# One written order for five engines: windowed attention and two gated layers on one core

## The chip, the cores and the metric

The kernel runs on one core of a Trainium2 chip. The core has a matmul engine (TensorE, PE in the profile, with its weight loads as PEld), a vector engine (VectorE, DVE), an activation engine (ScalarE, ACT), a general engine (GpSimd, POOL) and a queue that issues the transfers (SyncE, SP). Each engine works through its own list of instructions; between engines they wait for one another by semaphores. The metric is the device time of one execution in microseconds (us), lower is better; several runs are taken and their median stands.

## The reference

Two batches of 768 positions go through three stages one after the other: attention over chunks of 32 positions with a small context and 8 memory keys, a layer with a position-mixing gate, and a layer with a 3-tap convolution and a sigmoid gate. All inputs are f32.

```
# attention, 8 heads of 64: chunk of 32, 16 to the left, 8 to the right, 8 memory keys
scores = scale * matmul(q_c, k_full.T); scores -= max(scores)
a = exp(scores); a /= sum(a) + 1e-9; out_c = matmul(a, v_full)
# first layer
h = gelu_tanh(x @ w_in)                  # [2, 768, 512] @ [512, 1024]
u, v = h[..., :512], h[..., 512:]
v_n = (v - mean(v)) / sqrt(var(v) + 1e-6) * g_ln
v_s = einsum('ts,bsd->btd', w_sg, v_n) + b_sg[None, :, None]
x = x + (u * v_s) @ w_out
# second layer
h = relu(x @ w_in2)                      # [2, 768, 512] @ [512, 1024]
gate = sigmoid(conv over 3 positions of h with conv_w)
y = (h * gate) @ w_out2
```

Note that `einsum('ts,bsd->btd')` mixes all 768 positions of one batch: the mix of a batch needs the normalised v of all its positions, and no others.

## The kernel before

**Tiles and stages.** The 1536 positions are cut into 12 tiles of 128; tiles 0 to 5 are batch 0, tiles 6 to 11 batch 1. For a tile, `qk` makes the scores on PE (64 small f32 matmuls), `rows_max` takes the maximum off on DVE, `ex` is the exponential on ACT, `pt` turns the result, `pv` multiplies by the values, `x_of` divides by the sum, `xt` turns the tile once more. From then on every f32 product is made of three f16 products: each operand is scaled by a power of two found from its own absolute sums (`abs_sum`, `top_of`, `scale_from`), and `split` makes a high half (ACT) and a low half (DVE, or POOL for the pieces listed in `PC`, `PX` and `PK`). `mm3` (line 157) issues the three matmuls. `V` is the v half of `x @ w_in` (12 matmuls of 512 columns a tile), `U` the u half (48 of 128 columns), `N` the normalising of three tiles, `M` the mix (18 matmuls of 384 columns for each of 16 pieces), `O` the product with w_out (12 of 384 columns, 16 pieces), `I` the product with w_in2 and its convolution (24 of 384 columns, 16 pieces), `G` the scale of a batch's gate, `H` its split (one 768-column block a piece, 8 pieces a batch) and `Y` the last product (24 of 512 columns for each of 12 tiles).

**Weights.** They arrive as 64-bit floats; `narrow` makes f32 of a 128x512 piece by three DVE operations that follow from each other (lines 105, 107, 109). There are 28 such pieces.

**Order.** Two strings, `FIRST` and `SECOND`, give the order in which steps are recorded; what the engines then get is decided by a scheduler (`schedule_with_timeline_sim=True`) on all engines but SP, which keeps the written order. The weights of the second half (`w_out`, `w_in2`, `w_out2`) are recorded as `jobs` that `pump` deals out between the steps of `SECOND`. `FIRST` holds the attention, V, U and N of all 12 tiles; after it a pool of PSUM banks and a pool of attention buffers are closed (`p1.close()`) and others take their place, and the transfer of `b_sb` behind that point, with the raw weights of the second half after it, waits until the closed buffers are free. `SECOND` runs the M and O of both batches, then the I, G, H and Y.

## Time and profile before

| what | value |
|---|---|
| runs | 389.77 us median of 3 (389.65 to 391.6) |
| the profiled execution | 391.75 us, of which 389.0 us span from the first to the last instruction |
| PE, DVE, ACT, POOL busy | 334.4, 236.5, 219.5, 74.4 us |
| PE instructions | 3658 matmuls |
| moved by DMA | 35.22 MB |

Read it so: the span is what the program itself takes; the 2.75 us beside it lie before the first and after the last instruction. A busy engine is not one at its peak: PE's records overlap, and the granted clock of its matmuls has two levels, 1.2 and 2.4 GHz, shown as a share of the upper one.

### The profile page before, as it was taken

How to read it: one execution, taken by the hardware profiler on the slowest of the kernel's cores; microseconds unless marked ns; L12 is line 12 of the kernel's file. 1: busy time of each engine (PE TensorE's matmuls, PEld its weight loads, DVE VectorE, ACT ScalarE, POOL GpSimd, SP SyncE). 2: the span in 40 equal slices, each digit the busy share in tenths (PEclk: the TensorE clock that was granted, in tenths of full speed). 3: DMA queues.
4: the chain of work that ended last, by engine and by line, in shares of the span. 5: the costliest groups of instructions: out<-in, count | busy, mean ns of one | idle time of the engine just before them, and what ended most of it. 6: DMA issues, size and time to landing. Idle time of an engine off the chain costs nothing.

```text
span 389.0 us, 8771 instructions
## 1 busy us (share of the span) xinstructions
PE 334.4 (86%) x3658; PEld 205.3 (53%) x3658; DVE 236.5 (61%) x467; ACT 219.5 (56%) x439; POOL 74.4 (19%) x194
## 2 busy tenths in 40 slices
PE   6357789949489799799999999999984999997996
PEld 6233356748347366366666665666641455553445
DVE  1983656222864153649988889969998964338000
ACT  1456556863825555345554669689669773447111
POOL 1026204401600054333000105401006100000000
PEclk9658899978969899899999999999996999998999
DMA  7994072671012002530330410510210010000021
GB/s 268 406 369 131 3 241 63 245 252 29 31 56 56 2 3 85 174 112 0 110 108 2 163 56 1 167 51 0 70 41 0 2 55 29 27 27 29 27 81 54
DMA packets 13783, 35.22 MB, mean 91 GB/s; under 512 B 1968, under 2 KB 2224, under 8 KB 13744
## 3 DMA queue, kind: packets, MB, share of 16 engines
q1 hardware_dynamic: 13744, 34.67, 25.5%
q8 instruction: 28, 0.46, 0.5%
q14 instruction: 11, 0.09, 0.1%
HBM read 31.52 MB, written 3.15 MB: 89 GB/s over the span
## 4 chain that ended last, share of the span: by engine, by line
PE 54%; DVE 16%; DMA 11%; ACT 10%; issue 4%; POOL 3%; SPq 1%; ACTq 0%; DVEq 0%
PE o L157 20%; PE mx L157 12%; PE vps L157 8%; PE i L157 5%; PE ups L157 4%; DMA raw<-in_w_out_dram 3%; DMA sgVS<-in_w_sgt_dram 2%; DMA ruWSG<-in_w_in_dram 2%; DMA vwa<-in_vw_dram 2%; DVE c L690 2%; ACT h L686 1%; DVE wsg L149 1%; DVE gate L695 1%; PE pv L296 1%; DVE c L692 1%
## 5 line engine op out<-in xcount | busy, mean ns | idle before, releaser
L157 PE MATMUL o<-wp,gsp 128*128 128x512 f16 (+1 forms) x312 | 66.0, 371 | 6.9 <-ACT gsp L143 6.9
L157 PE MATMUL i<-x2s,wi 128*128 128x384 f16 x384 | 66.9, 332 | 0.0
L157 PE MATMUL vps<-win,xs 128*128 128x512 f16 x144 | 42.7, 437 | 13.6 <-ACT xs L143 9.8
L157 PEld LDWEIGHTS <-wi 128*128 128x128 f16 x384 | 38.1, 99 | 27.5 <-issue 3.2
L157 PEld LDWEIGHTS <-gsp 128*128 128x128 f16 x312 | 30.8, 99 | 40.0 <-ACT gsp L143 8.0
L157 PE MATMUL mx<-wsg,vs 128*128 128x384 f16 x288 | 50.3, 331 | 0.0
L157 PEld LDWEIGHTS <-vs 128*128 128x128 f16 x288 | 28.3, 99 | 18.9 <-issue 1.4
L157 PE MATMUL ups<-xs,win 128*128 128x128 f16 x576 | 37.9, 222 | 0.0
L157 PEld LDWEIGHTS <-win 128*128 128x128 f16 x576 | 35.0, 100 | 4.3 <-issue 1.0
L157 PE MATMUL o<-gs,wo 128*128 128x384 f16 x192 | 34.6, 326 | 0.6 <-ACT gs L143 0.5
L157 PEld LDWEIGHTS <-xs 128*128 128x128 f16 x144 | 13.7, 108 | 30.7 <-ACT xs L143 12.0
L690 DVE SCALAR_TENSOR_TENSOR c<-h,cw_sb,c 128x768 f32<-128x768 f32 x16 | 16.3, 1017 | 16.9 <-ACT c L689 16.9
L361 DVE BATCH_NORM_STATS2 st<-v 128x6 f32<-128x512 f32 x12 | 8.3, 691 | 27.7 <-ACT v L359 27.7
L157 PEld LDWEIGHTS <-wo 128*128 128x128 f16 x192 | 18.6, 98 | 12.0 <-issue 0.2
L694 ACT ACTIVATE c<-c 128x768 f32<-128x768 f32 x16 | 13.4, 838 | 12.8 <-DVE c L692 12.8
L695 DVE TENSOR_TENSOR gate<-h,c 128x768 f32<-128x768 f32 x16 | 15.3, 956 | 8.5 <-ACT c L694 8.5
L720 ACT ACTIVATE o<-o,ixp0t 128x256 f32<-128x256 f32 x12 | 5.6, 470 | 21.8 <-issue 18.0
L359 ACT ACTIVATE v<-vps,ixv 128x512 f32<-128x512 f32 x12 | 8.2, 686 | 17.2 <-PE vps L157 17.1
L692 DVE SCALAR_TENSOR_TENSOR c<-h,cw_sb,c 128x768 f32<-128x768 f32 x16 | 16.3, 1017 | 0.7
L135 ACT ACTIVATE gs<-uf 128x384 f16<-128x384 f32 x16 | 8.3, 519 | 14.3 <-DVE uf L652 14.3
L135 ACT ACTIVATE xs<-xx 128x512 f16<-128x512 f32 x12 | 7.6, 629 | 13.3 <-DVE xx L311 13.3
L391 POOL TENSOR_TENSOR vs<-v,vs 128x512 f16<-128x512 f32 x12 | 14.1, 1193 | 5.3 <-ACT vs L390 5.3
(421 smaller groups left out, 567.3 us busy)
## 6 DMA issues: line engine op xcount, KB each, us to landing
raw<-in_w_out_dram SPq DMA_DIRECT2D x12, 512.0 KB, 3.5
vwSTG<-in_vw_dram SPq DMA_DIRECT2D x8, 520.0 KB, 3.7
raw<-in_w_in_dram SPq DMA_DIRECT2D x8, 512.0 KB, 3.5
q<-in_qt_dram SPq DMA_DIRECT2D x12, 256.0 KB, 5.3
kwb<-in_kw_dram SPq DMA_DIRECT2D x8, 368.0 KB, 6.1
out_dram<-o SPq DMA_DIRECT2D x11, 256.0 KB, 2.0
vwa<-in_vw_dram SPq DMA_DIRECT2D x4, 520.0 KB, 5.2
ruWSG<-in_w_in_dram SPq DMA_DIRECT2D x4, 512.0 KB, 9.9
```

The costliest lines, as they stand in the source:

```text
L135: nc.scalar.activation(room, src, AF.Abs, scale=2.0 ** (1 - EXP_TOP), accum_out=acc)
L149: nc.vector.scalar_tensor_tensor(out=lo, in0=src, scalar=sc[:, 0:1], in1=hi, op0=ALU.mult, op1=ALU.subtract)
L157: nc.tensor.matmul(ps, a, b, start=(i == 0), stop=(i == n - 1))
L296: nc.tensor.matmul(po[c * CH:(c + 1) * CH, par, hp * (D + 1):(hp + 1) * (D + 1)], t[rows, hp, c * CH:(c + 1) * CH], vw_t[i][rows, c, hp, : ...
L359: nc.scalar.activation(v, ps_t.pop(("v", i)), AF.Gelu_apprx_tanh, scale=inv_of(sc_x[i], i, "v"))
L361: nc.vector.bn_stats(out=st, in_=v)
L391: nc.gpsimd.tensor_tensor(out=lo[:, ib, :], in0=v, in1=hi[:, ib, :], op=ALU.subtract)
L690: nc.vector.scalar_tensor_tensor(out=c, in0=h[:, 0:S], scalar=cw_sb[:, f, 0:1], in1=c, op0=ALU.mult, op1=ALU.add)
L692: nc.vector.scalar_tensor_tensor(out=c, in0=h[:, 2:S + 2], scalar=cw_sb[:, f, 2:3], in1=c, op0=ALU.mult, op1=ALU.add)
L694: nc.scalar.activation(c, c, AF.Sigmoid)
L695: nc.vector.tensor_tensor(out=gate[b][f // 4][:, f % 4], in0=h[:, 1:S + 1], in1=c, op=ALU.mult)
L720: nc.scalar.activation(o[:, cs], ps[:, cs.start - cols.start:cs.stop - cols.start], AF.Copy, scale=inv_of(sc_g["gate", b], f"t{b}", f"p{h}"))
```

## The change

The kernel is rewritten around one table. `ORDER` is a string of some 1200 steps; `run` records each as it comes, all engines keep the recorded order (`manual_schedule()` without a list, and no scheduler), and each step is smaller than before: a step holds the work of one engine on one piece (`v.2.0` is the first three matmuls of V of tile 2, `cn.v.2` the narrowing of one piece of w_in's v half, `ms`/`mg`/`ma` the three operations behind a mix, `za` to `zd` the four behind the gate's scale). The mark `@` names the memory slot: PSUM is four single banks M0 to M3 and two pairs D0 and D1 for the whole program, and SBUF slots are reused by name, so nothing is closed in the middle. What the table does with the order:

- It goes batch by batch: attention, V, U and the normalising of batch 0, then its M and O among the attention, V and U of batch 1, then the I of batch 0 among the rest of batch 1, then the I of batch 1 among the Y of batch 0.
- The weights of the second half are loaded and narrowed among the steps of the first.

Other edits: the low halves that POOL made are made on DVE; so are the products of two scales (`product`, on POOL before as `inv_product`); x is split from its f32 copy in SBUF and no longer from PSUM; the high and low halves of g and y (`gh`, `gl`, `yh`, `yl`) are made two blocks at a time (768 elements a row where there were 384); the exponential is one tile at a time where before groups of one to three tiles had one call; q and k of a tile are one transfer; the 20 small buffers for maxima are set once at the start; 50 warming matmuls instead of 70; the last tile is no longer cut in two.

```diff
-FIRST = """
-Z q0 e0 c0 q1 e1 c1 b0 c2 c3 s0 q2 q3 e2 x0 k0 k1 k2 k3 b1 x1 c4 c5 V0 c6 c7 s1 b2 V1 x2 k4 k5 k6 k7 q4 q5 e3
...
+ORDER = """
+lv.0 lq.0 W@M0 lv.2 lq.2 lq.1 lv.1 lw.v.2 lw.v.0 lg lw.v.3 qk.0@D0 mx.0 lq.3 sb.0 lw.v.1 qk.2@D1 mx.2 ex.0 sb.2 lq.5
...
+    def product(self, out, a, b):
+        self.nc.vector.tensor_tensor(out=out, in0=a[:, 1:2], in1=b[:, 1:2], op=ALU.mult)
...
+    def split_hi(self, hi, src, sc):
+        self.nc.scalar.activation(hi, src, AF.Copy, scale=sc[:, 0:1])
...
+    def cn(self, w, j):
+        self.narrow(self.f32(w, j), self.raw(w, j))
...
+    def ex(self, i):
+        self.nc.scalar.activation(self.s(i), self.s(i), AF.Exp, scale=0.125)
...
+    def v(self, i, k):
+        b, ts = self.ts(i)
+        xh, xl = self.xs(b)
+        wh, wl = self.hilo("v")
+        self.mm3(self.bank(f"vp{i}"), [(xh[:, k, ts], xl[:, k, ts], wh[:, k, FF:], wl[:, k, FF:])], k == 0, k == KD - 1)
...
+    def gh(self, g, j):
+        b, ts = self.gsl(g)
+        js = slice(2 * j, 2 * j + 2)
+        self.split_hi(self.gs(b)[0][:, js, ts], self.uf(b)[:, js, ts], self.sc(f"g{g}"))
...
+    def run(self, token):
+        name, _, self.slot = token.partition("@")
+        fn, *args = name.split(".")
...
+    ctx.enter_context(tc.manual_schedule())
...
+    for token in ORDER.split():
+        steps.run(token)
...
-    with _tile.TileContext(nc, schedule_with_timeline_sim=True) as tc:
+    with _tile.TileContext(nc) as tc:
```

Three places show what moved. The first is PE where the mix of batch 0 begins. Before, its first matmuls (`mx0_0`) follow those of V and U of tile 11 (`vps11`, `ups11`), the last tile of batch 1:

```order
L157 LDWEIGHTS xs10_1494
L157 MATMUL vps11_2446<-win0_97,xs10_1494 128x512
L157 LDWEIGHTS xs10_1494
L157 MATMUL vps11_2446<-win1_98,xs10_1494 128x512
L157 LDWEIGHTS win0_97
L157 MATMUL ups11_2466<-xs10_1494,win0_97 128x128
L157 LDWEIGHTS vs00_1184
L157 MATMUL mx0_0_2579<-wsg0_1028,vs00_1184 128x384
```

Now matmuls of the mix (`mx1.1` and `mx0.2`, both of batch 0) stand around the attention of tiles 11, 7, 8 and 10 of batch 1 (`pp` turns, `po` is the product with the values, `sc` the scores):

```order
L234 LDWEIGHTS vs01_1158
L234 MATMUL mx1.1_1755<-wsg0_835,vs01_1158 128x384
L462 MATMUL pp11_1762<-ident_71,sring_231 128x128 x4
L476 MATMUL po7_1768<-vw7_878,ptr_311 32x65 x32
L462 MATMUL pp8_1806<-ident_71,sring_231 128x128 x4
L437 MATMUL sc10_1818<-qk10_1104 32x64 x32
L234 LDWEIGHTS vs00_1157
L234 MATMUL mx0.2_1854<-wsg0_835,vs00_1157 128x384
```

The mix of batch 0 moved ahead of most of batch 1's attention, V and U.

The second place is DVE at the start. Before, after its first memset, the three operations that narrow a piece of w_in (lines 105, 107, 109) are mixed with those of the next piece and of tile 0's scores:

```order
L105 TENSOR_SCALAR tvXS10_101<-rvUF1_99 128x512
L107 SCALAR_TENSOR_TENSOR tvXS10_101<-rvUF1_99,tvXS10_101 128x512
L267 TENSOR_REDUCE mx0_240<-sc0_204 128x8
L109 SCALAR_TENSOR_TENSOR tvXS10_101<-rvUF1_99,tvXS10_101 128x512
L105 TENSOR_SCALAR tvXS10_101<-rvUF1_99 128x512
L272 TENSOR_TENSOR s0_242<-sc0_204,mx0_240 128x2x4x64
L107 SCALAR_TENSOR_TENSOR tvXS10_101<-rvUF1_99,tvXS10_101 128x512
```

Now the scores of three tiles come first, and the three operations of a piece (lines 250, 252, 253) follow each other:

```order
L449 TENSOR_REDUCE mx_227<-sc0_194 128x8
L453 TENSOR_TENSOR sring_231<-sc0_194,mx_227 128x2x4x64
L449 TENSOR_REDUCE mx_227<-sc2_234 128x8
L453 TENSOR_TENSOR sring_231<-sc2_234,mx_227 128x2x4x64
L449 TENSOR_REDUCE mx_227<-sc1_278 128x8
L453 TENSOR_TENSOR sring_231<-sc1_278,mx_227 128x2x4x64
L250 TENSOR_SCALAR tv1_356<-rawv1_188 128x512
L252 SCALAR_TENSOR_TENSOR tv1_356<-rawv1_188,tv1_356 128x512
L253 SCALAR_TENSOR_TENSOR tv1_356<-rawv1_188,tv1_356 128x512
```

The first narrowing moved from the head of the queue to behind six operations on scores.

The third place is PE where the scale of batch 0's gate is made. Before, its two small matmuls (`gt0t`) and those of a weight (`wp1t`) are followed at once by a matmul that reads the split gate (`gsp000`), and the product with w_in2 of batch 1 (`i22_3`) stands behind it:

```order
L118 MATMUL wp1t_3768<-ident_78,wap1_3710 4x128
L118 MATMUL gt0t_3861<-ident_78,gacc0_3424 16x128
L120 LDWEIGHTS ones_bf_83
L120 MATMUL wp1t_3768<-wp1r_3769,ones_bf_83 128x1
L120 LDWEIGHTS ones_low_85
L120 MATMUL gt0t_3861<-gt0r_3862,ones_low_85 128x1
L157 LDWEIGHTS gsp000_3870
L157 MATMUL o20_0_0_4009<-wp0_3357,gsp000_3870 128x512
L157 LDWEIGHTS gsp000_3870
L157 MATMUL o20_0_0_4009<-wp1_3358,gsp000_3870 128x512
L157 LDWEIGHTS wi0_2861
L157 MATMUL i22_3_4044<-x2s10_3302,wi0_2861 128x384
```

Now the second of them (`zt0`, from the reduced `rz0`) is followed by matmuls of the product with w_in2 of batch 1 (`h1.3`, then `h1.0`):

```order
L263 LDWEIGHTS ones_low_78
L263 MATMUL zt0_3681<-rz0_121,ones_low_78 128x1
L234 LDWEIGHTS i00_2289
L234 MATMUL h1.3_3673<-x2s10_3369,i00_2289 128x384
L234 LDWEIGHTS i00_2289
L234 MATMUL h1.3_3673<-x2s11_3370,i00_2289 128x384
L234 LDWEIGHTS i01_2290
L234 MATMUL h1.3_3673<-x2s10_3369,i01_2290 128x384
```

Between the gate's scale and the first matmul that reads the split gate there are now 30 matmuls of batch 1's product.

## Rows read from the trace of the kernel before

**Rows 1.** First part of the page: busy time, share, instructions.

```profile
PE 334.4 (86%) x3658; PEld 205.3 (53%) x3658; DVE 236.5 (61%) x467; ACT 219.5 (56%) x439; POOL 74.4 (19%) x194
```

**Rows 2.** Stretches: length, busy of PE, PEld, DVE, ACT, POOL, clock, DMA, GB/s.

```profile
0.00:33.00 33.00, 17.12 (x473) 13.98 (x474) 21.46 (x48) 14.41 (x30) 7.23 (x20) 0.73 0.90 329
33.00:160.00 127.00, 101.59 (x1925) 69.82 (x1924) 57.77 (x149) 70.98 (x112) 35.04 (x100) 0.90 0.27 91
160.00:290.00 130.00, 129.24 (x827) 77.92 (x825) 111.83 (x219) 84.13 (x205) 22.80 (x52) 0.99 0.22 74
290.00:298.00 8.00, 0.81 (x4) 0.37 (x5) 6.60 (x14) 7.23 (x14) 3.48 (x8) 0.82 0.00 1
298.00:345.00 47.00, 47.00 (x240) 23.95 (x239) 27.80 (x27) 27.60 (x54) 5.47 (x15) 0.96 0.08 29
345.00:353.00 8.00, 6.03 (x30) 2.67 (x29) 3.85 (x7) 4.61 (x8) 0.33 (x2) 1.00 0.09 33
...
386.00:389.00 3.00, 0.00 (x0) 0.00 (x0) 0.00 (x0) 0.18 (x1) 0.00 (x0) 1.00 0.13 44
```

**Rows 3.** Whom PE waited for: us in total, times, longest us.

```profile
PE vps L157 <- ACT xs L143: 9.8, 6, 3.9
PE o L157 <- ACT gsp L143: 6.9, 2, 5.7
```

**Rows 4.** The chain that ended last: start us, us, what.

```profile
27.20 3.02 POOL tvXS L146
...
32.91 3.65 PE vps L157 x10
...
90.80 2.17 PE vps L157 x10
...
135.76 2.73 PE ups L157 x47
...
151.77 5.47 DMA raw<-in_w_out_dram
...
209.19 2.92 PE mx L157 x18
...
323.19 3.90 PE i L157 x24
327.09 5.18 PE o L157 x24
```

**Rows 5.** Groups of instructions: name, shapes, count; busy us, mean ns; idle before.

```profile
L107 DVE SCALAR_TENSOR_TENSOR tp<-raw,tp 128x512 int32<-128x512 int32 x8 | 5.3, 686 | 0.1
L105 DVE TENSOR_SCALAR tp<-raw 128x512 int32<-128x512 int32 x8 | 3.2, 423 | 1.8 <-DMA raw<-in_w_out_dram 1.7
L149 DVE SCALAR_TENSOR_TENSOR wo<-to,wos,wo 128x512 f16<-128x512 f32 x4 | 2.8, 745 | 0.3 <-ACT wo L143 0.3
L361 DVE BATCH_NORM_STATS2 st<-v 128x6 f32<-128x512 f32 x12 | 8.3, 691 | 27.7 <-ACT v L359 27.7
L272 DVE TENSOR_TENSOR s<-sc,mx 128x512 f32<-128x512 f32 x12 | 8.2, 680 | 0.6 <-PE pp L284 0.6
L650 DVE SCALAR_TENSOR_TENSOR mt<-mx,gsc,b_sb 128x384 f32<-128x384 f32 x16 | 9.7, 611 | 0.4 <-POOL vs L391 0.4
L690 DVE SCALAR_TENSOR_TENSOR c<-h,cw_sb,c 128x768 f32<-128x768 f32 x16 | 16.3, 1017 | 16.9 <-ACT c L689 16.9
L359 ACT ACT_TABLE_LOAD x3 | 3.8, 1283 | 2.2 <-PE vps L157 2.2
L143 ACT ACTIVATE wo<-to,wos 128x512 f16<-128x512 f32 x4 | 2.6, 711 | 0.0
```

**Rows 6.** Timeline of DVE, 8 to 11 us: start us, us, instruction.

```profile
8.57 0.43 DVE L105 TENSOR_SCALAR tvXS<-rvUF 128x512 int32<-128x512 int32 x1 [7.63 <-DMA rvUF<-in_w_in_dram]
...
9.64 0.68 DVE L267 TENSOR_REDUCE mx<-sc 128x8 f32<-128x512 f32 x1
10.24 0.68 DVE L109 SCALAR_TENSOR_TENSOR tvXS<-rvUF,tvXS 128x512 int32<-128x512 int32 x1
```

More of the change, by code (lines that the diff above doesn't have):

```diff
@@ L64, in fused_kernel @@
[L64 to L96 removed]
+WARM = 50
@@ new lines, in top_all, with scale_from @@
+    def top_all(self, red, t, low=False):
+        self.nc.tensor.matmul(t[:, P:P + 1], self.ones_low if low else self.ones, red, start=True, stop=True)
+    def scale_from(self, sc, t):
+        r = t[:, P:P + 1]
+        v = self.nc.vector
+        v.tensor_scalar(out=sc[:, 0:1].bitcast(I32), in0=r.bitcast(I32), scalar1=0x7F800000,
+                        scalar2=0x7F800000, op0=ALU.bitwise_and, op1=ALU.bitwise_xor)
+        v.tensor_scalar(out=sc[:, 1:2].bitcast(I32), in0=sc[:, 0:1].bitcast(I32), scalar1=-1.0,
+                        scalar2=float(254 << 23), op0=ALU.mult, op1=ALU.add)
@@ L519, in fused_kernel @@
-    nc.sync.dma_start(g_sb, g_ln.rearrange("(k p) -> p k", p=P), allow_slow_non_contiguous=True)
-    nc.sync.dma_start(cw_raw, conv_w)
-    def warm():
-        z = const.tile([P, P], F16, tag="zero", name="zero")
-        nc.vector.memset(z, 0.0)
-        ps = mmps1("warm")
-        for _ in range(WARM):
-            nc.tensor.matmul(ps[:, :P], z, z, start=True, stop=True)
-    def front(gi):
-        for i in GROUPS[gi]:
-            qk(i)
-            rows_max(i)
-        ex(gi)
-    def back(i):
-        pt(i)
-        pv(i)
-        x_of(i)
-        x_scale(i)
-        xt(i)
-        xt_split(i)
@@ L615, in fused_kernel, with pov @@
-    small[0] = lambda name: psm.tile([P, 512], F32, tag="mm", name=name)
-    gs, x2s, gate, gsp, gacc = {}, {}, {}, {}, {}
-    def gslice(g):
+                for par, rows in enumerate(self.ROWS):
+                    self.nc.tensor.matmul(po[c * CH:(c + 1) * CH, par, hp * (D + 1):(hp + 1) * (D + 1)],
+                                          t[rows, hp, c * CH:(c + 1) * CH], v[rows, c, hp, :],
+                                          start=True, stop=True)
+    def pov(self, i):
+        return self.bank(f"po{i}")[:, :, 0:4 * (D + 1)].rearrange("p a (h k) -> p a h k", h=4)
@@ new lines, in u, with inv, iv @@
+    def u(self, i, j):
+        b, ts = self.ts(i)
+        xh, xl = self.xs(b)
+        wh, wl = self.hilo("u")
+        cs = slice(j * P, (j + 1) * P)
+        self.mm3(self.bank(f"up{i}")[:, cs], [(wh[:, k, cs], wl[:, k, cs], xh[:, k, ts], xl[:, k, ts])
+                                              for k in range(KD)], True, True)
+    def inv(self, a, b):
+        return self.small(f"i{a}{b}", 1)
+    def iv(self, w, i):
+        self.product(self.inv(f"x{i}", w), self.sc(f"x{i}"), self.sc("w" + w))
@@ new lines, in p, with pe, st @@
+    def p(self, b, t, f):
+        ts = slice(t * P, (t + 1) * P)
+        gh, gl = self.gsp(b, f)
+        wh, wl = self.hilo("p0")
+        self.mm3(self.p2(b, t), [(gh[:, ts], gl[:, ts], wh[:, f], wl[:, f])], f == 0, f == KF2 - 1)
+    def pe(self, b, t):
+        o, ps = self.row(f"o{b}.{t}"), self.p2(b, t)
+        for h in range(2):
+            cs = slice(h * 256, (h + 1) * 256)
+            self.nc.scalar.activation(o[:, cs], ps[:, cs], AF.Copy, scale=self.inv(f"z{b}", f"p{h}"))
+    def st(self, b, t):
+        self.nc.sync.dma_start(self.out[b, t * P:(t + 1) * P], self.row(f"o{b}.{t}"))
```

1060 lines of the change are left out of this document (521 added, 539 removed).

## The prediction

> **What bounds the kernel now.** I began with the busy times: PE is busy for 334.4 us of the span of 389.0 and DVE for 236.5 [rows 1], so PE comes first, but 54.6 us pass in which it has nothing to do. The table by stretches shows where, and that is the view to look at longest. In the first 33 us PE works 17.1 us while the transfers run at 329 GB/s and DVE is busy 21.5 us. From 33 to 160 us, where the attention, V and U of all 12 tiles are done, no engine is near its limit: PE 101.6 of 127 us (25.4 us idle, mean granted clock 0.90), ACT 71.0, DVE 57.8. From 160 to 290 us PE is full (129.2 of 130) and DVE is busy 111.8. Then 7.2 us are lost between 290 and 298, 2.0 between 345 and 353, and 3.3 at the end [rows 2]. The waits name who ended this: V waits for the split x (9.8 us in 6 waits), the last product for the first block of the split gate (5.7 us at once) [rows 3]. In the first stage each tile is one long chain through PE, DVE and ACT, and there is too little other work to put between; in the second stage there is plenty.
>
> How much work PE has at the upper clock follows from the chain, where runs without a gap show the spacing of matmuls: 18 of the mix take 2.92 us (0.162 each), 24 of w_in2 3.90, 24 of w_out2 5.18 (0.216), 10 of V 2.17, 47 of U 2.73 (0.058) [rows 4]. So 144 matmuls of V cost 31.2 us, 576 of U 33.4, 288 of the mix 46.7, 192 of w_out 31.2 (as w_in2), 384 of w_in2 62.4, 288 of w_out2 62.2: 267 us. The attention and the small matmuls I take at 35 us and the warming at 4. That makes about 306, in a span of 389.0.
>
> **The change part by part.** The matmuls stay what they were; the order, the engine of some steps and the waits change. I cut the new order in six stages and add up each engine's rows in it. The largest of the three sums is the least time a stage can take.
>
> DVE prices: narrowing one piece 1.79 us (0.423 + two of 0.686), a low half 0.745, an operation on 768 elements 1.02 (a low half of that size too), statistics 0.86 (0.691 and the short step behind it), an operation on scores 0.68, one behind the mix 0.61; ACT: a high half 0.71 [rows 5]. The small ones (0.15 to 0.36) are counted in.
>
> 1. *To the first matmul of V.* Two turns cost opposite ways. The scores of three tiles now go ahead of the first piece of w_in, and their transfers too: 6.1 MB must land before the last v piece is there, at 329 GB/s [rows 2] 18.5 us. Behind that stand two narrowings (3.6), an absolute sum, four operations on scores (2.7), the scale, three of the division, one high and one low half: some 12 us, so 31 us. On the other hand the low halves are no longer on POOL, where one such step held the chain for 3.02 us [rows 4]. I take 31, as before, when the steady V began at 32.9 us [rows 4], but with four tiles' value products done instead of two. Bounds 29 and 34.
> 2. *To the first matmul of the mix* (24 three-matmul steps of V, 22 twelve-matmul steps of U). DVE: 5 narrowings 9.0, 13 low halves 11.2, 6 statistics 5.2, the rest of the attention, the normalising and small ones 21.9: **47.3 us**. PE 39, ACT 38.9 with five loads of a function table.
> 3. *To the first product with w_out*: PE **36.8** (24 six-matmul steps of the mix 23.4, attention, V and U of batch 1 13.4), DVE 26.2.
> 4. *To the first product with w_in2*: DVE **37.1** (6 narrowings 10.8, 8 low halves 6.7, w_out's 8 results 4.9, the rest 14.7), PE 33.4.
> 5. *To the scale of batch 0's gate*: PE **91.0** (37 steps of w_in2 36.1, 24 of the mix 23.4, 16 of w_out 15.6, 14 of U 9.8, 8 of V 5.2, small ones), DVE 88.4, ACT 71.5.
> 6. *To the last matmul*: PE **88.8** (96 three-matmul steps of w_out2 62.2, 27 of w_in2 26.3), DVE 42.8.
>
> Sum 31 + 47.3 + 36.8 + 37.1 + 91.0 + 88.8 = 332.0; with the 3.3 us behind the last matmul [rows 2] 335.3.
>
> What stages lose beyond the sum no row of before shows, so I bound it by the nearest stretches. Below: 160 to 290 us, PE idle 0.6% [rows 2]. Above: 33 to 160 us, 20%. Stages 2 and 4 are led by DVE with PE and ACT close behind; the nearest is the start, where DVE, once it had its first data at 8.6 us [rows 6], was busy 21.5 of 24.4: 12% lost, so 10.1 us on 84.4. Stage 3 is PE's with much other work to hand, I take a third of the 20%, 7%: 2.6 us. Stages 5 and 6 are like 160 to 345, almost no idle time and a granted clock of 0.96 to 0.99 [rows 2]: 2%, 3.6 us. On the other side DVE rows overlap: operations of 0.68 us start 0.60 apart when they don't follow from each other [rows 6]. By that the DVE stages would be up to 8% shorter (6.8 us), but the three steps of a narrowing now stand behind each other; I take half, 3.4. Span: 335.3 + 10.1 + 2.6 + 3.6 - 3.4 = 348.2. The profiled execution had 2.75 us outside its span and lies 2.0 above the median of the runs, so the median should be **349 us**.
>
> Edits that I cost at nothing: the transfers of the second half's weights, which before came so late that one of 5.47 us ended the chain at 157 us [rows 4], are spread under stages 2 to 5, where DMA was 22% busy [rows 2]; if one is late, DVE waits for about as long, and PE behind it. At batch 0's gate 30 matmuls of w_in2 (4.9 us) stand in front of the first reader of the split gate; before it six DVE steps have to end (two small ones, one product, three low halves, 4.6 us); if that cover were gone the 5.7 us of [rows 3] would be back. The 20 fewer warming matmuls lie in a wait for data.
>
> A wait is added too: with one fixed order per engine, whatever stands behind a late step waits, ready or not. On DVE the division of a tile stands between narrowings; if the value product is late, the weights are late, and V with them. That is in the 12%.
>
> ACT changes its function table 17 times instead of 9, since exponentials, gelus and sigmoids of two batches mix. A load's row is 1.28 us [rows 5], so stage 2 on ACT is 38.9 + 6.4 = 45.3 us, still under DVE's 47.3. The Trainium skill, page "ScalarE: Activation LUTs", section "What ACT_TABLE_LOAD costs", speaks against this change: a switch costs 2.66 us with the drain that follows, and functions should be grouped by table; by that figure stage 2 would be 52.2 us on ACT and my estimate 4.9 us more.
>
> **The rivals.**
> - *Everything covers.* If the fillers work as from 160 to 290 us, the loss is 0.6% of 301 us: 335.3 + 1.8 - 3.4 = 333.7, median 334.5. For it: that stretch. Against: DVE is as loaded as PE in stages 2, 4 and 5.
> - *The chains stay.* If stages 2 to 4 lose the 20% of 33 to 160 us (24.2), stage 5 half of that share (9.1) and stage 6 2% (1.8), the span is 370.4, the median 371. For it: the tiles' chains have the same steps, and in a fixed order nothing overtakes. Against: there is twice the work to hand.
> - *ACT leads stage 2*: if each table load takes twice its row, ACT needs 51.7 us there, 4.4 more than DVE: 353.
> - *Slower: the clock.* In stages 2 to 4 PE has 109 us of work at the upper clock, broken by waits. Before, with 20% idle, the granted clock there was 0.90, and 0.73 in the broken first 33 us [rows 2]. At a mean of 0.60 this work takes 73 us more, of which 12 fit into the slack of stages 2 and 4: 410 us. It decides from a mean of 0.67, where 53 us more, less the 12, eat the forecast's gain of 41. Against it: nothing in before was so low outside the start. The Trainium skill's page "TensorE: Matmul & The Clock Gate", section "What's actually happening", says that the lower level is the default and activity lifts it, which is the direction of this rival.
>
> That the change does not do what it says is no rival: the order in the built program shows it.
>
> **How the numbers follow.** Chances: the forecast, 340 to 358 us, 0.52; everything covers, 332 to 340, 0.15; the chains stay, 358 to 385, 0.19; ACT leads 0.05 (within the forecast's span of times); the clock, slower, 0.06; the clock only so far that it ends near 390, 0.03. The range 332 to 371 leaves out the clock's 0.09, some 0.05 of the chains above 371 and 0.04 below 332. Half a per cent is about what runs of this kernel can tell from no change (their three lie within 0.5%): faster 0.91, same 0.03, slower 0.06.
>
> **What would show it.** The first steady V at about 31 us; the mix before 90 us, where now it starts at 160; DVE busy over 85% from 31 to 160 us where it was 45%; PE idle under 30 us in all; no wait over 2 us of w_out2's product for the split gate; 17 table loads of 1.28 us. The prediction is wrong if PE's idle time from 31 to 160 us stays near 20%, if the granted clock there falls under 0.8, or if V starts after 40 us.

## The result and the profile after

The changed kernel takes **361.12 us** (median of 4 runs, 360.44 to 361.37) against 389.71 us on the same chip: 0.926 of the time before, 95% interval 0.922 to 0.930. The forecast was 349, with a range of 332 to 371. Its profiled execution took 360.44 us, with a span of 358.6. The span fell by 30.4 us: PE was idle for 21.3 us less and busy for 9.1 less. Some 6 of the 9.1 are its clock, an estimate: before, 40.1 us of its busy time lay in stretches at the lower level (granted clock 0.50, 1.2 GHz), now 27.8, and 3.4 us at that level made stage 5 about 1.6 us longer (see the rows for stage 5 below).

The first lines of the page after, busy times and their shares, answer to [rows 1]:

```profile
PE 325.3 (91%) x3614; PEld 200.1 (56%) x3614; DVE 251.5 (70%) x501; ACT 223.8 (62%) x437; POOL 36.1 (10%) x96
PEclk9555799998999999999999899999999999999999
```

Next the table by stretches of the kernel after, cut where the forecast cut its six stages (the last stretch ends 0.5 us behind the last matmul; start:end and length, then PE, PE's weight loads, DVE, ACT and POOL busy with their instructions, granted clock, DMA share, GB/s). It answers to [rows 2]:

```profile
0.00:40.99 40.99, 27.51 (x732) 21.61 (x733) 23.01 (x53) 15.96 (x32) 1.66 (x28) 0.63 0.96 372
40.99:86.42 45.43, 40.79 (x816) 28.87 (x814) 41.39 (x102) 40.08 (x66) 12.79 (x30) 1.00 0.42 143
86.42:127.02 40.60, 39.32 (x561) 25.29 (x561) 27.71 (x64) 25.08 (x52) 2.95 (x4) 0.96 0.26 80
127.02:161.38 34.36, 33.92 (x386) 21.94 (x385) 31.23 (x83) 28.07 (x59) 1.58 (x5) 1.00 0.24 78
161.38:263.61 102.23, 93.90 (x671) 58.25 (x669) 86.34 (x152) 67.53 (x141) 17.13 (x30) 0.98 0.13 42
263.61:355.10 91.49, 89.88 (x456) 44.14 (x453) 41.80 (x53) 46.54 (x88) 0.00 (x0) 1.00 0.08 29
```

The stages against the forecast, in us. "With losses" adds to each term its own share (12% on stages 2 and 4, 7% on 3, 2% on 5 and 6); the column adds up to 351.7, from which the forecast took 3.4 off for overlapping rows. The last column is the same kernel in a later run (e12), to show what moves by itself:

| stage | term | with losses | after | after, again |
|---|---|---|---|---|
| 1, to the first V product | 31.0 | 31.0 | 41.0 | 41.4 |
| 2, to the first mix | 47.3 | 53.0 | 45.4 | 47.4 |
| 3, to the first w_out product | 36.8 | 39.4 | 40.6 | 42.3 |
| 4, to the first w_in2 product | 37.1 | 41.6 | 34.4 | 34.4 |
| 5, to batch 0's gate scale | 91.0 | 92.8 | 102.2 | 100.6 |
| 6, to the last matmul | 88.8 | 90.6 | 91.0 | 91.0 |
| behind it | 3.3 | 3.3 | 4.0 | 4.0 |

So the start is 10 us longer than forecast and stage 5 is 9.4, while stages 2 and 4 together are 14.8 shorter. What moves by itself in stages 2 and 5 goes with PE's granted clock. It was 1.00 in stage 2 here and 0.91 in e12, and in stage 5 the other way round. These two rows stand for stage 5, first a stretch of the kernel after, then the whole stage in e12:

```profile
196.80:200.20 3.40, 3.34 (x19) 2.24 (x19) 2.79 (x5) 0.36 (x1) 0.00 (x0) 0.50 0.00 0
165.40:266.00 100.60, 92.27 (x671) 57.24 (x669) 86.25 (x152) 67.62 (x142) 17.12 (x30) 1.00 0.13 43
```

PE's idle time in the stage is 8.33 us in both (102.23 less 93.90, and 100.6 less 92.3), so it is the better measure of what a change does there.

**The start.** PE's timeline of the kernel after, the rows that begin after an idle time that no engine and no transfer explains ("issue"); in brackets its length:

```profile
12.58 0.65 PE L437 MATMUL sc<-qk 64*32 64x64 f32 x24 [0.85 <-issue]
19.52 0.68 PE L476 MATMUL po<-vw,ptr 64*32 64x65 f32 x29 [2.53 <-issue]
34.80 1.08 PE L476 MATMUL po<-vw,ptr 64*32 64x65 f32 x52 [1.76 <-issue]
40.77 0.38 PE L526 MATMUL px<-ident,xx 128*128 128x128 f32 x2 [1.22 <-issue]
```

The first three are in the middle of a product of 64 small matmuls, whose operands were there (40, 35 and 12 of 64 done), the fourth between the second and the third of four transposes. Counted from PE's first matmul, they stand behind 222, 349, 603 and 730 matmuls: 127, 254 and 127 apart, which is 254 or 508 instructions with their weight loads. The DMA view of the same kernel for 32 to 35 us names a queue of its own for instructions (queue, kind: packets, MB, share of 16 engines):

```profile
DMA packets 340, 1.21 MB, mean 402 GB/s; under 512 B 25, under 2 KB 25, under 8 KB 339
q1 hardware_dynamic: 339, 1.19, 100.8%
q8 instruction: 1, 0.02, 2.2%
```

One block of code comes in while the data queue fills the engines. The packets of this queue that come ahead of the four stops begin at 10.1, 17.1, 32.3 and 38.4 us, and each time PE goes on 2.3 to 2.5 us later. That makes a suspect: code that stands behind data.

**Stage 5.** POOL's and VectorE's timeline of the kernel after, batch 1's inverse square root and what runs beside it:

```profile
163.06 1.04 POOL L590 TENSOR_TENSOR vt<-vt,va 128x3 f32<-128x3 f32 x1
...
165.02 0.19 POOL L590 TENSOR_TENSOR vt<-vt,va 128x3 f32<-128x3 f32 x1
...
167.38 4.13 POOL L606 TENSOR_TENSOR vs<-v,vs 128x512 f16<-128x512 f32 x3 [1.32 <-ACT vs L601]
...
166.10 0.55 DVE L596 TENSOR_SCALAR v<-v,mv,vy 128x512 f32<-128x512 f32 x1 [1.80 <-POOL vy L593]
...
167.75 1.38 DVE L596 TENSOR_SCALAR v<-v,mv,vy 128x512 f32<-128x512 f32 x1
...
170.53 1.53 DVE L252 SCALAR_TENSOR_TENSOR ti<-raw,ti 128x512 int32<-128x512 int32 x1
172.09 0.69 DVE L253 SCALAR_TENSOR_TENSOR ti<-raw,ti 128x512 int32<-128x512 int32 x1
```

The same step of 3 columns takes 0.19 us on POOL when VectorE stands still (from 164.3 to 166.1) and 1.04 when it works; VectorE's passes of 0.55 and 0.69 take 1.38 and 1.53 while POOL makes low halves (167.38 to 171.51). And PE's timeline there has seven stops, 8.05 us together with the 0.64, 1.45, 0.95 and 0.51 that are not shown:

```profile
167.89 2.98 PE L234 MATMUL vp<-win,xs 128*128 128x512 f16 x13 [1.16 <-DVE xs L288]
187.76 0.34 PE L234 MATMUL mx3.2_2750<-wsg,vs 128*128 128x384 f16 x1 [1.11 <-POOL vs L606]
196.86 1.44 PE L234 MATMUL up<-xs,win 128*128 128x128 f16 x12 [2.23 <-DVE mt3.2_2936 L629]
```

My theory was therefore: code fetches make the start late, the chain on POOL makes stage 5 late. Rivals: late data at the start, the order itself in both, and VectorE's load in stage 5.

### The profile page after: what moved, and what is told of

The parts are those of the page before. It is cut to its first block, busy times and chain, and to the rows that moved or that the text cites. A ratio compares the mean times of both kernels' runs of the same rounds, so it can differ in the third digit from the quotient of the medians.

```text
span 358.6 us, 8520 instructions
## 1 busy us (share of the span) xinstructions
PE 325.3 (91%) x3614; PEld 200.1 (56%) x3614; DVE 251.5 (70%) x501; ACT 223.8 (62%) x437; POOL 36.1 (10%) x96
## 4 chain that ended last, share of the span: by engine, by line
PE 59%; DVE 21%; ACT 8%; issue 4%; POOL 4%; DMA 2%; SPq 0%; ACTq 0%; DVEq 0%
PE vp L234 4%; PE up L234 3%; PE e0.2_4005 L234 3%; PE e1.2_4124 L234 3%; PE sc L437 2%; PE po L476 2%; PE pp L462 2%; DMA qk<-in_qk_dram 2%; DVE ti L252 2%; ACT hb L732 2%; DVE v L596 1%; PE o21.1_4209 L234 1%; PE o21.3_4202 L234 1%; PE o21.2_4217 L234 1%; PE o21.0_4190 L234 1%
## 5 line engine op out<-in xcount | busy, mean ns | idle before, releaser
L234 PEld LDWEIGHTS <-i 128*128 128x128 f16 x384 | 37.2, 98 | 26.9 <-issue 2.2
L234 PE MATMUL up<-xs,win 128*128 128x128 f16 x576 | 37.0, 221 | 4.2 <-DVE mt3.2_2936 L629 2.2
L740 DVE SCALAR_TENSOR_TENSOR cb<-hb,cw,cb 128x768 f32<-128x768 f32 x32 | 31.7, 1014 | 11.8 <-ACT cb L737 11.7
L234 PE MATMUL vp<-win,xs 128*128 128x512 f16 x144 | 35.8, 379 | 1.2 <-DVE xs L288 1.2
L234 PEld LDWEIGHTS <-wo 128*128 128x128 f16 x192 | 18.7, 98 | 12.4
L745 ACT ACTIVATE cb<-cb 128x768 f32<-128x768 f32 x16 | 13.4, 840 | 17.0 <-DVE cb L740 16.7
L748 DVE TENSOR_TENSOR gate<-hb,cb 128x768 f32<-128x768 f32 x16 | 15.2, 956 | 4.0 <-ACT cb L745 3.9
L476 PE MATMUL po<-vw,ptr 64*32 64x65 f32 x768 | 12.4, 253 | 5.4 <-issue 4.3
L288 DVE SCALAR_TENSOR_TENSOR gsp<-gate,scz,gsp 128x768 f16<-128x768 f32 x16 | 15.4, 1013 | 1.8 <-ACT gsp L280 1.8
L280 ACT ACTIVATE gsp<-gate,scz 128x768 f16<-128x768 f32 x16 | 13.9, 928 | 1.3 <-DVE scz L268 1.3
L737 ACT ACTIVATE cb<-hb,cw 128x768 f32<-128x768 f32 x16 | 14.6, 933 | 0.2
```

Of the source, the lines that this page charges most:

```text
L234: self.nc.tensor.matmul(ps, a, b, start=first and i == 0, stop=last and i == n - 1)
L280: self.nc.scalar.activation(hi, src, AF.Copy, scale=sc[:, 0:1])
L288: self.nc.vector.scalar_tensor_tensor(out=lo, in0=src, scalar=sc[:, 0:1], in1=hi, op0=ALU.mult, op1=ALU.subtract)
L476: self.nc.tensor.matmul(po[c * CH:(c + 1) * CH, par, hp * (D + 1):(hp + 1) * (D + 1)], t[rows, hp, c * CH:(c + 1) * CH], v[rows, c, hp, :] ...
L737: self.nc.scalar.activation(self.c(f), self.h(f)[:, 1:S + 1], AF.Copy, scale=self.cw[:, f, 1:2])
L740: self.nc.vector.scalar_tensor_tensor(out=self.c(f), in0=self.h(f)[:, 2 * side:S + 2 * side], scalar=self.cw[:, f, 2 * side:2 * side + 1], ...
```

## The experiments

Times below are medians, ratios are to the kernel before on the same chip. The changed kernel stands at 0.926 and, in e12, at 0.927 (0.923 to 0.931).

**e1. The small steps on VectorE.**

```diff
-        pool = self.nc.gpsimd        # in np(), 13 steps for each group
+        pool = self.nc.vector
```

> Only the 13 small steps of each group's inverse square root go from GpSimd to VectorE. Theory (chain on GpSimd, made longer by sharing with VectorE): in the changed kernel these steps took 6.3 us for group 2 and 5.5 us for group 3, 0.39 to 1.04 us each, in front of batch 1's mix; on VectorE they should take about 2.5 us a group, VectorE's neighbours there (the conversion passes of 0.69 us that took 1.5) go back to their usual length, the stretch from the first w_in2 product to batch 0's gate scale falls from 102.2 to 95-99 us, median 354-358. Rival (VectorE itself is the limit in 160-200, 88% busy, and 52 more steps come on top): that stretch stays at 101-105 us, median 360-366. Rival (the three row buffers hold the gelus of the next tiles back until the low halves are done): the gain is 2 us at most, median 359-361.

Measured 364.26 us, 0.932 (0.928 to 0.935). Stage 5 took 101.5, stage 2 48.3 us (45.4 and 47.4 in the two profiles of the changed kernel). The theory got nothing it asked for; the time and stage 5 are in the ranges of the first rival, VectorE's load. PE's idle time in stage 5 was 7.9 instead of 8.3 us.

**e2. The low halves of v on VectorE too.**

```diff
-        self.nc.gpsimd.tensor_tensor(out=lo[:, ib, :], ...)     # in vl()
+        self.nc.vector.tensor_tensor(out=lo[:, ib, :], ...)
```

> The 13 small steps and the 12 low halves of the normalised rows both go from GpSimd to VectorE, so that GpSimd does nothing there. Theory (sharing): a low half takes about 0.7 instead of 1.42 us and no VectorE pass is longer than 1.0 us in 160-200; that stretch is at least as short as with the steps alone, median 351-357. Rival (VectorE's load decides): 12 more passes of 0.7 us are 8 us more of VectorE's work, half of them in front of batch 0's mix where VectorE already led (45.4 us stage with 41.7 of 47 us busy); median 361-369.

Measured 360.69 us, 0.922 (0.918 to 0.925). The sharing is real. VectorE's groups of the changed kernel, where POOL works beside them (last columns: busy us, mean ns):

```profile
L252 DVE SCALAR_TENSOR_TENSOR to<-raw,to 128x512 int32<-128x512 int32 x4 | 4.4, 1110 | 0.1
L252 DVE SCALAR_TENSOR_TENSOR ti<-raw,ti 128x512 int32<-128x512 int32 x8 | 6.4, 797 | 0.3
```

and the same groups of e2, where it does not:

```profile
L251 DVE SCALAR_TENSOR_TENSOR to<-raw,to 128x512 int32<-128x512 int32 x4 | 2.8, 692 | 0.1
L251 DVE SCALAR_TENSOR_TENSOR ti<-raw,ti 128x512 int32<-128x512 int32 x8 | 5.5, 693 | 0.3
```

But it isn't what the stages cost: stage 5 became 99.9, and stage 2, led by VectorE, rose to 48.8 (VectorE busy 45.8 us, where it was 41.4). The work taken off POOL lengthens the engine that leads.

**e5. Both for batch 1 alone.**

```diff
+        pool = self.nc.vector if g >= 2 else self.nc.gpsimd      # in np()
+        eng = self.nc.vector if b else self.nc.gpsimd            # in vl()
```

> As the run with the small steps and the low halves on VectorE, but only for batch 1's two groups; batch 0's stay on GpSimd. Theory (the chain of batch 1's normalising costs, batch 0's hid it and VectorE was full there): the stage to the first mix is back at 45.4 us (48.7 with all on VectorE), the stage to batch 0's gate scale keeps its 99.9 (102.2 in the changed kernel); 2 to 3 us faster than the changed kernel, ratio to the kernel before about 0.919. Rival (the 2.3 us there were only the later start of that stage, its VectorE work having been done before): that stage goes back to 102 and the ratio is 0.926.

Measured 360.35 us, 0.921 (0.916 to 0.927): stage 2 45.9, stage 5 99.9, as the theory said, though the interval holds 0.926. PE's idle time in stage 5 fell from 8.3 to 6.4 us. Against e12 the stage is only 0.8 us shorter, because e5 has a stretch of 3.4 us at 0.50 in it and e12 has none. In stage 5 the stops only changed their place: 2.44 us of PE's wait for a step of tile 11 that now stood behind the 13 small ones, 2.15 for a low half. So the chain on POOL isn't the cause of the 9.4 us; 1.9 of them hang on it.

**e7. Low halves of weights on GpSimd**, 14 of them.

```diff
- wl.s.* wl.o.* wl.i0.*      (VectorE, one pass)
+ wm.s.* wm.o.* wm.i0.*      (GpSimd, two passes)
```

> One part undone: the low halves of the gate weights, of w_out and of w_in2's first half (14 of them) are made on GpSimd, in two passes each, as in the kernel before. If VectorE's length alone leads the stages to the first mix and to the first w_in2 product, they become shorter by their six (1.0 us each) and eight (0.75 us) passes less: 39-41 and 29-31 us, ratio 0.90. My theory (sharing: VectorE's passes beside GpSimd's work take up to twice as long, and the low half itself takes two slow passes): the mix starts no earlier, 46-52 us, the sum is 0-10 us slower than the changed kernel, ratio 0.927-0.95.

This is not a part of the change undone, as the expectation has it. In the kernel before, these 14 were made on VectorE in one pass too, as [rows 5] shows for w_out and its view by tiles for the other two:

```profile
L149 DVE SCALAR_TENSOR_TENSOR wsg<-sgUF,wsgs,wsg x4: 1003/1005/2025, 102.5 to 106.9; 128x768 f16<-128x768 f32 x4
L149 DVE SCALAR_TENSOR_TENSOR wi<-ti,wi0s,wi x4: 744/748/753, 206.7 to 209.7; 128x512 f16<-128x512 f32 x4
```

What the change did move from GpSimd are four low halves of w_in, two of w_out2 and those of four tiles of x; no run moves these back.

Measured 375.62 us, 0.961 (0.954 to 0.968): 14 us slower than the changed kernel, more than the theory's 0 to 10. Stages 2 to 5 took 49.1, 45.6, 37.2 and 104.1. POOL's groups in e7:

```profile
L285 POOL TENSOR_TENSOR wsg<-ts,wsg 128x768 f16<-128x768 f32 x6 | 10.2, 1704 | 0.5
L284 POOL TENSOR_SCALAR ts<-ts,scws 128x768 f32<-128x768 f32 x6 | 6.1, 1020 | 0.1
```

A low half of 768 columns takes 2.7 us here against about 1.0 on VectorE, and PE waits 5.4 us ahead of the mix and 2.6 for a low half of w_out. VectorE's shorter list did not help: stage 2 got longer although VectorE was busy for 37.8 us in it instead of 41.4. So e7 prices GpSimd for this work; it does not say what the change earned.

**e3. Transfers later.** SyncE's order; `cn.u.1`, `ca.u.1` and `ca.s.0`, which read these pieces, go behind too.

```diff
- lb lq.4 lv.3 lv.5 lc lw.u.2 lw.u.0 lw.u.1 ls.1 ls.0 lq.6 lq.7 lq.8 lw.u.3 lv.4
+ lq.4 lv.3 lv.5 lv.4 lw.u.1 lw.u.0 lw.u.3 lw.u.2 lc ls.0 ls.1 lq.6 lb lq.7 lq.8
```

> Eleven transfers that nothing needs before about 42 us (w_in's other half, the gate weights, the bias, the taps, q and k of tiles 6 to 8) are issued behind v of tile 4, which has to wait for a product at about 34 us; the three VectorE and ScalarE steps that read them first go later in the order. Theory (TensorE's stops in the middle of a product are instruction fetches that stand behind saturated transfers): with quiet transfers between 21 and 34 us the stop at 33.0 (1.76 us) falls below 0.5 us, the one at 39.6 (1.22) shrinks too, and the first V product comes at 37-39.5 instead of 41.0; median 358-360. Rival (a fetch takes its 2.5 us whatever the transfers do, and short products outrun it): the stops stay within 0.4 us of their length and the first V product at 40-41.5. Rival (data was late): the first V product comes earlier by more than 4 us with the stops as long as before.

Measured 363.26 us, 0.930 (0.925 to 0.936): no gain in all, but the question is answered. PE's timeline of e3 where the stop of 1.76 us had been:

```profile
33.15 1.34 PE L475 MATMUL po<-vw,ptr 64*32 64x65 f32 x64 [0.43 <-DVE sring L452]
34.41 0.19 PE L262 MATMUL wtv<-rv,ones 128*128 128x1 bf16 x1
```

All 64 products in one run; the stop at 39.6 is gone as well. The DMA view of e3 from 29 to 33 us:

```profile
DMA packets 1, 0.02 MB, mean 4 GB/s; under 512 B 0, under 2 KB 0, under 8 KB 0
q8 instruction: 1, 0.02, 1.4%
```

The block of code is the only packet in 4 us. It begins at 30.1 us, where it began at 32.3 for the same place in the program of the changed kernel. The two early stops, where transfers are still full, stayed (1.78 and 2.99 us), and where e3 moved the transfers to, a new one came: 1.10 us at 62.6, in the scores of a later tile, behind 1111 matmuls (222 and seven times 127), with the transfers at 101%. One more of 1.13 us at 156.8 follows 64 small products, with the transfers at 79% (154 to 155 us). In all four PE went on 2.4 to 2.5 us after the packet began. The first V product came at 37.7 us, but the mix at 90.6: q and k of later tiles now came late, and PE waited 4.46 us for them at 65 us.

**e4. Fewer warming instructions.**

```diff
- WARM = 50:  matmul(ps[:, :P], self.zero, self.zero)
+ WARM = 13:  matmul(ps, self.zero[:, :P], self.zero)      # zero is 512 wide
```

> The 50 warm-up products of 128 columns become 13 of 512 (the same time on TensorE, 74 instructions fewer ahead of everything). Theory (the stops lie at fixed counts of TensorE's instructions, every 256, where the next block of code has to come): each stop moves 74 instructions (37 products) later in the program: from 40 products into the scores of tile 1 to 9 products into pv of tile 0, from 35 products into pv of tile 2 to just behind it, from 12 products into pv of tile 1 to 49 products into it, from the middle of px of tile 3 of the changed kernel into the V products behind it. Rival (the stops wait for something in the program, a transfer or a buffer): they stay at the same products. Time: theory 359-362, since the stops only move; under the rival 361.

Measured 358.78 us, 0.917 (0.914 to 0.920). PE's timeline of e4, again the rows behind "issue":

```profile
14.72 1.11 PE L475 MATMUL po<-vw,ptr 64*32 64x65 f32 x55 [1.99 <-issue]
28.08 0.44 PE L436 MATMUL sc<-qk 64*32 64x64 f32 x9 [0.67 <-issue]
34.56 0.47 PE L475 MATMUL po<-vw,ptr 64*32 64x65 f32 x15 [2.23 <-issue]
```

The stop in the scores of tile 1 has gone to 9 products into the value product of tile 0 (55 left), that in the value product of tile 1 from 12 to 49 products (15 left). These two stand where the theory put them, so the stops are tied to the count of instructions, not to the program. Of the other two expected nothing is seen, and one of 0.67 shows 55 products into the scores of tile 4. It fits the count: the three stand behind 222, 476 and 603 matmuls, where the changed kernel has 222, 349, 603 and 730. They add up to 4.9 instead of 6.4 us, the first V product came at 38.4, the mix at 84.0.

**e8. Wide warming and a milder delay of transfers.** `lw.u.3 ls.0 ls.1 lc lq.6 lq.7 lb lq.8` go behind `lv.4`, nothing else moves.

> The 13 wide warm-up products together with a milder delay of transfers: three of the four pieces of w_in's other half stay early, and only its last piece, the gate weights, the taps, the bias and q and k of tiles 6 to 8 go behind v of tile 4. No step of the engines moves. Theory (stops only where a fetch meets full transfers; in the run with the later loads the loss after the first V product came from u's narrowing): the stops at 28 and 34 us of the run with fewer warm-up products (0.67 and 2.23 us) go or fall below 0.5, the first V product comes at 35.5-37.5 (38.4 there), the stage to the first mix stays at 45-47, ratio 0.907-0.914. Rival (what that stage gains it gives back, VectorE being its bound): V earlier, first mix at 84 as there, ratio 0.915-0.919.

Measured 359.00 us, 0.918 (0.912 to 0.925), the same as e4. The stop of 2.23 us at 34 is gone; the one at 28 stayed (1.17), its packet having begun at 26.6 under full transfers; the one at 13 was 2.76. First V product at 37.6, first mix at 84.4: what the start gained, stage 2 gave back (46.9). Part of that is the delay's own doing: PE waited 1.67 us, until 63.7, for q and k, which e4 did not.

**e6. Moves in the order between 160 and 200 us.** For each engine the tokens that change places:

```diff
 ACT, DVE: - vn.8 vn.6 ... xh.11 xl.11        + xh.11 xl.11 vn.8 vn.6
 ACT:      - vg.10 ca.i1.2 vg.9 ca.i1.3 vg.11 + vg.10 vg.9 vg.11 ca.i1.2 ... ca.i1.3
 DVE:      - cn.i1.3 vb.9 yl.1.1 vb.11 yl.1.0 nr.3  + vb.9 vb.11 nr.3 yl.1.1 yl.1.0 cn.i1.3
 DVE:      - hs (four) ms.3.2 ms.3.1          + hs (two) ms.3.2 ms.3.1 hs (two)
```

> Only places in the written order change, all between the first w_in2 products and the first conversion of w_out2 of the changed kernel: x of tile 11 is split ahead of the normalising instead of behind its first two rows; the gelus of tiles 9 and 11 stand ahead of ScalarE's sums of two weight pieces; statistics and the square root of group 3 ahead of one narrowing and two low halves of x2; batch 1's first two mix results ahead of half the convolution. Theory (the stops of TensorE in 160-200, 1.16, 0.64, 1.45, 0.95, 1.11, 0.51 and 2.23 us, come from what stands ahead in the order of the other engines): at least four of the seven go, TensorE is busy for over 36 of the 40 us (31.95 now), ratio 0.909-0.916. Rival (GpSimd's slow steps decide, wherever they stand): the stops of 0.95 and 1.11 stay, the gain is 2-3 us, ratio 0.918-0.921. Rival (VectorE's load decides the stretch): the stops come back later in the stretch, ratio 0.923-0.930.

Measured 359.63 us, 0.919 (0.912 to 0.926); stage 5 took 99.4 us, with PE idle for 6.8 instead of 8.3. The stops of 1.16, 0.64 and 1.45 are gone and the 2.23 became 0.50, but the low halves on POOL are now waited for at the first mix products of group 3 as well (1.22 and 0.90), 0.89, 1.11 and 0.52 stayed, and 1.23 for the next mix result came anew. PE was busy for 33.46 of the 40 us, not 36. The rival of GpSimd's slow steps describes it best, in the ratio too.

**e9. All three together**, and batch 0's first two mix results ahead of a narrowing.

```diff
 DVE: - cn.o.1 cn.o.3 ms.0.0 ms.1.0   + cn.o.1 ms.0.0 ms.1.0 cn.o.3     (ca.o.3 behind cn.o.3)
```

> The moves in 160-200, the 13 wide warm-up products and the milder delay of transfers together, and one more move: the first two mix results of batch 0 go ahead of the fourth narrowing of w_out, for which TensorE waited 2.63 us at about 92 us. Batch 1's normalising stays on GpSimd. If the parts add up: first V product at 37.6, the stage to the first mix 46.5, the next 40.0-40.8 (42.2 in the run with the moves alone), 34.4, 99.3, 90.6: span 353-354.5, median 355-356.5, against 361.1 of the changed kernel. Rival (each engine has little slack left, a move only hands its wait on): the stage behind the first mix stays at 42 us and the median at 357-359.

Measured **353.65 us**, 0.905 (0.901 to 0.909). Its stages: 36.1, 46.9, 38.8, 34.4, 99.4 and 91.0. The median is below the theory's 355 to 356.5. More than the sum was found in stage 3, 3.5 us less than in e12 for a wait that fell from 2.64 to 0.84. The reason is in the table by stretches. Of the changed kernel again (e12), with the wait in the first stretch:

```profile
93.00:98.20 5.20, 2.56 (x16) 1.44 (x15) 4.74 (x9) 2.17 (x6) 0.00 (x0) 1.00 0.62 209
98.20:101.60 3.40, 3.40 (x14) 1.67 (x12) 0.54 (x4) 0.00 (x0) 0.00 (x0) 0.50 0.42 143
101.60:105.00 3.40, 3.40 (x23) 2.03 (x22) 0.62 (x1) 0.00 (x0) 0.00 (x0) 1.00 0.02 5
```

and of e9, around the shorter wait:

```profile
86.00:89.90 3.90, 3.08 (x19) 1.75 (x18) 3.81 (x6) 1.25 (x3) 1.00 (x1) 1.00 0.45 161
89.90:94.00 4.10, 4.08 (x26) 2.46 (x26) 2.66 (x8) 0.91 (x4) 0.00 (x0) 1.00 0.63 227
```

After the stop PE was given the lower level (0.50, 1.2 GHz) for 3.4 us and did 14 matmuls in them where it does 23 at the upper one; after the shorter stop it kept the upper level. Here a stop was paid nearly twice: 1.8 us less of waiting gave 3.5. It is not always so. The same stop of 2.6 us was followed by 0.50 in e4, e5, e6 and e8 as well, but not in e3; the one of 2.23 us in stage 5 was in the first profile of the changed kernel, but not in e3, e4, e8 and e12.

**e10. The scale of w_in earlier; batch 1's normalising on VectorE in an order written for it.**

```diff
 PE:  - qk.4 wta.v qk.5 pp.3 pv.1 wtc.v       + wta.v qk.4 wtc.v qk.5 pp.3 pv.1      (v.2.0 ahead of px.1)
 DVE: - xl.0 mx.4 mx.5 sb.4 wtb.v sb.5 xl.2 wtd.v   + xl.0 wtb.v cn.u.1 mx.4 wtd.v mx.5 sb.4 sb.5 wl.v.0 xl.2
 DVE: - cn.i1.2 ... cn.i1.3 ... cn.p0.* (four) ahead of the mix results
      + vn vl vb nr np of batch 1 without a narrowing between, cn.p0.* and cn.p1.* behind, to 225 us
```

> The same warm-up products, transfers and early mix results; in the start, the scale of w_in's first half goes ahead of the scores of tile 5 and of the value product of tile 1 (in the changed kernel behind them), its high halves ahead of the next exponentials, and one narrowing of the other half into VectorE's wait at 28-30 us; in 160-200, batch 1's normalising is wholly on VectorE and the order there is written for it: tile 11's small steps first, then root, rows and low halves without a narrowing between, the narrowings of w_out2 behind. Theory (what stands ahead in the order holds the start): the scale is known at about 30 instead of 34 us, first V product at 34-36.5, first mix at 81-83.5 (84.4 with the transfers alone). Rival (VectorE's work sets the mix, not the scale): first V earlier, first mix still at 84-85. In 160-200, theory (order plus sharing): TensorE's stops there fall from 8 to under 4 us, the stage to batch 0's gate scale 95-98 us. Rival (VectorE's load): 99-101. Median 349-355 if both theories hold, 355-358 if neither.

Measured 364.59 us, 0.933 (0.929 to 0.936): 11 us slower than e9, and a miss on both counts. VectorE's timeline of e10 shows the first, the narrowing that was put into a gap:

```profile
30.46 0.43 DVE L249 TENSOR_SCALAR tu<-rawu 128x512 int32<-128x512 int32 x1 [2.92 <-DMA rawu<-in_w_in_dram]
```

Its piece had not landed, and in one fixed order everything behind it waited too; with 4.42 us of PE's wait for q and k, which end at 67 us, the first mix came at 89.0. In stage 5 the stops between 160 and 200 fell, but that stage took 106.8 us: 2.77 us for a low half of x2 at 179, and then 1.71, 1.58 and 2.10 between 200 and 227, where the narrowings had been moved to. VectorE was busy 89.5 us there; its work can be moved, not hidden.

**e11. The scale early without that narrowing; the third mix result of batch 1 earlier; two of the twelve low halves on VectorE**, all on top of e9.

```diff
 ACT: - ex.4 pt.3 ex.5 pt.4 wh.v.0 xa.1 ... wh.v.1 wh.v.2 wh.v.3   + wh.v.0 wh.v.1 ex.4 pt.3 wh.v.2 wh.v.3 ex.5 pt.4
 DVE: - hs.0.0.0 hs.0.0.1 ms.2.2              + ms.2.2 hs.0.0.1 hs.0.0.0
+        eng = self.nc.vector if i in (7, 10) else self.nc.gpsimd       # in vl()
```

> The run with moves, warm-up products and transfers, and three things more: the scale of w_in's first half and its high halves early as in the run before, but without the narrowing that waited 2.92 us for its piece there; the third mix result of batch 1 also ahead of the second half of the convolution (TensorE waited 1.23 us for it at 192 us); the low halves of tiles 7 and 10 on VectorE, the other ten on GpSimd. Theory (in order, and what is asked first is ready): the scale at about 29.5 us, first V product at 34-35.5 (36.1), the first mix 1 us earlier, stage to batch 0's gate scale 97-98.5 (99.4), median 350-352.5 against 353.65. Rival (the mix is set by VectorE's work, the scale isn't what holds it): first V earlier, first mix at 83, only the last stage gains, median 352-354.

Measured 353.13 us, 0.904 (0.900 to 0.908): as e9. The scale was known at 29.4 us instead of 32.6 in e9, but the first V product came at 35.9 and the mix at 84.2: the scale isn't what the mix waits for. That it is VectorE's work, as the rival says, is not shown, since PE waited 3.48 us for q and k, until 62.5 (1.70 in e9). Stage 5 fell to 98.7, with PE idle for 4.8 us instead of 6.8; the rest of that went to 3.4 us at 0.50, which e9 did not have.

**e12. The changed kernel again**, beside e11.

> The changed kernel as it is, on the same chip as the run before it, so that the two can be compared without the kernel before: 360.5-363 us.

Measured 362.15 us. So e9 and e11 are 8.5 to 9 us (2.4%) faster than the changed kernel.

## Why the prediction was right, and where it was not

The direction, the mechanism and the range held: with one order over both batches PE was idle for 33.3 us (358.6 less 325.3) instead of 54.6, the mix began at 86.4 instead of 160, and from 31 to 160 us PE was busy 119.3 of 129 us. V's waits for the split x, 9.8 us in [rows 3], shrank to one in the page after:

```profile
L234 PE MATMUL vp<-win,xs 128*128 128x512 f16 x144 | 35.8, 379 | 1.2 <-DVE xs L288 1.2
```

That the order did this is read from the two profiles. No run keeps the other edits and undoes the order, so how the gain divides between them is not shown.

Of the 12 us that are missing from the point, 10.4 are in the span (358.6 against 348.2); the rest is that the profiled execution now lay 0.7 us below the median, where the forecast took 2.0 above. In the span two terms were too small by 19.4 us and two too large by 14.8. That they nearly cancel is luck; by its own mark for stage 1, V after 40 us, the prediction failed there.

1. *Stage 1, 31 us, measured 41.0.* The step that failed is the "some 12 us" behind the transfers: a sum of VectorE's and ScalarE's work, with nothing for PE's. The 18.5 us for the transfers were nearly right. The four v pieces in the kernel after, with their issue (first and last start) and the time to landing:

```profile
L359 SPq DMA_DIRECT2D rawv<-in_w_in_dram x4: 328/428/452, 3.7 to 8.8; - x4
...
DMA to landing us min/median/max: 10.4/11.6/12.0
```

   The last had landed by 20.8 us. There were 15.4 us from there to the scale (36.2). VectorE was busy for 12.4 of them; 2.1 more it waited for a product of the weight's sums that stands behind PE's value product, the one with the stop of 1.76 us. Then PE had a value product and two more sets of transposes to do before its turn at V. Stops for code are 6.4 us of PE's time; taking away some (e3, e4, e8) brought the first V product to 37.6 to 38.4. Before shows no such stop, though its transfers took 90% of the first 33 us [rows 2]; why is not shown. That data was late is refuted by e3, in which the same pieces came no earlier. Beyond that it is PE's own work ahead of V in the order, at the lower level: in e9 PE was busy for 7.6 of the 8.0 us before V at 36.1, with the attention of other tiles, at 0.50. So the early scale (e11) moved V by 0.2 us only.
2. *Stages 2 and 4, 53.0 and 41.6 us with their losses, measured 45.4 and 34.4.* Two steps failed the same way. VectorE's work was summed from durations of single rows, 47.3 and 37.1; it was busy for 41.4 and 31.2, 12 and 16% less. Its rows in the two stages add up to 46.3 and 34.8, so 8.5 us of the difference are rows that overlap, and by 3.3 the sum itself was too high. I had seen the overlap and taken half of it, 3.4 us. And the loss was 9% (41.4 of 45.4) in stage 2, though 12% in e12, at the lower clock; stage 4 was led by PE, 33.9 of 34.4, not by VectorE.
3. *Stage 3*, 39.4 forecast, 40.6 and 42.3: right, with some 1.7 us lost in each to a stretch of 3.4 us at the lower level.
4. *Stage 5, 92.8 us, measured 102.2 and 100.6.* PE's work was right (93.9 and 92.3 busy, 91.0 summed). The 2% for losses failed: 8.3 us were idle, 8.1 of them between 160 and 200, where I had taken 160 to 345 of the kernel before as the nearest stretch. There batch 1's gelus, normalising, low halves and mix stand in series among w_in2's work. It's neither POOL alone (e5) nor these places in the order alone (e6): they took 1.9 and 1.5 us off PE's idle time, moves and part of the low halves together (e11) 3.6, and with VectorE at 86 of 102 us a step moved away was missing elsewhere (e10). Of the 4.8 us that e11 leaves, 2.3 are waits for low halves on GpSimd (1.22 and 1.11).
5. *Stage 6 and the end*, 93.9 forecast, 95.0: right. The cover at batch 0's gate worked: w_out2's first product follows at 270.1 us without a wait, so the 5.7 us of [rows 3] did not come back.

**The rivals.** "The chains stay" (371) and "everything covers" (334) are both refuted by the idle 7.5% between 31 and 160 us. "ACT leads stage 2" is refuted by ACT's timeline of the kernel after:

```profile
51.69 0.71 ACT L280 ACTIVATE xs<-xf,scx 128x512 f16<-128x512 f32 x1
52.42 1.28 ACT L566 ACT_TABLE_LOAD   x1
53.71 0.69 ACT L566 ACTIVATE v<-vp,ix1v 128x512 f32<-128x512 f32 x1
```

A switch costs its row, 1.28 us, and the next activation begins at once. The figure of 2.66 us that the Trainium skill gives (page "ScalarE: Activation LUTs", section "What ACT_TABLE_LOAD costs") is not seen here; the measurement decides. There were 17 loads, as forecast. "The clock" came true in the small: 0.50 from about 10 to 40 us, and for 3.4 us after some single stops, with a mean of 0.946.

Of what I named as signs, the mix before 90 us, the 17 loads and the cover came; VectorE's 82% from 31 to 160 (85 asked), PE's 33.3 us idle (30 asked) and V at 41.0 (the mark for "wrong" was 40) did not, and the last pointed to the right place.
